# The results of two chunks go into the place of chunk 1's rows, and the third chunk is loaded meanwhile

## Chip, cores and metric

One core of one Trainium2 chip. The metric is the device time of one execution in microseconds; times of a kernel are medians over runs.

## What is computed

Three layers, cut to what matters here:

```python
def reference(q, k, v, w_in, w_out, w_gate, w1, w2):
    a = attn(q, k, v)              # 4 batches x 8 heads, 576 positions, width 64:
                                   # pooled attention (mean of 4) plus a band of |i-j| < 4
    x = a.transpose(0, 2, 1, 3).reshape(2304, 512)
    h = x @ w_in                   # 512 -> 2048
    g = np.where(h >= 1, h, np.where(h <= -1, 0.0, (h + 1) ** 2 / 4))
    x = g @ w_out                  # 2048 -> 512
    # then 8 experts with 288 rows each: the logits x @ w_gate, all of them
    # sorted, set which row goes to which expert
    return experts(x, w_gate, w1, w2)   # relu(x @ w1[e]) @ w2[e] for its rows
```

## The kernel before, in words

The program is written as many small generators (`pooled`, `local`, `prep`, `up`, `down`, `gates`, `flush` and so on). While the program is built, a planner in `run` keeps a modelled clock for each engine and lets the generator go on that is due first; what it yields says on which engine its next piece goes (`"P"` TensorE, `"A"` ScalarE, `"V"` VectorE, `"G"` GpSimd, `"N"` none) or what it has to wait for: a condition on marks (`done("x", c)`), a PSUM bank, or a named place (`need(..., "xio")`). `CAPS` says how many places of each name there are; of `xio` there is one. So the order of the instructions on each engine is fixed when the program is built, and on the chip an engine takes its instructions in that order and waits on semaphores. The order of SyncE is also that of all loads and stores (`dma`, L104 to L108).

All instructions of an engine are written by one helper each: L106 issues transfers, L120 matmuls, L124 transposes, L128 ScalarE, L141 VectorE and GpSimd.

In the first part of the run three things are interleaved: the attention (16 pairs of heads, `pooled` and `local`; its results are written to `x_cols` in DRAM, column by column), the preparation of the weights (`prep`, which splits each of 16 blocks of `w_in` and `w_out` into a high and a low part), and the second layer in chunks of 256 rows of x. The first seven chunks run here, two more go together behind them.

A chunk goes so. `load_chunks` loads its columns from `x_cols` into `xio` (L717) and splits them: ScalarE copies the high part into `xts` (L723), VectorE or GpSimd subtracts for the low part (`low_part`, L707). `xts` has two tiles, for even and odd chunks. `gemm1` then makes one of 16 blocks of h, 12 matmuls of 128x256 in one half of PSUM bank 0; `gates` makes g of it (two `gar` on ScalarE, then VectorE, GpSimd or both, then `ghi` and `glo`). The product with `w_out` follows.

Chunks 0 and 1 run side by side (`up` and `down`), since the weights come block by block: their results fill banks 1 to 4, two for each chunk. `flush_first` scales them into `xio` (L643 to L647), writes them to `x_rows`, transposes them, and computes the logits from them (`mark("logits", c)`); only at its end it gives `xio` back (L668). From chunk 2 on `gemm` drives the blocks: `gemm1` of block n and `gemm2` of block n - 2 (`LAG` at L40), whose results lie in banks 1, 2 and 3. `gemm2` of chunk c waits for `done("flush", c - 1)` (L764), so that of chunk 2 waits until chunk 1's banks have been emptied. `load_chunks` loads chunk 2 when chunk 0 has passed its 16 blocks and `xio` is free (L712).

After the chunks come the last rows, the routing, and the eight experts, which are not touched.

Of the kernel before, what the change touches and what calls it, by code (L numbers as in the profile page):

```python
# [11 lines left out]
F32 = mybir.dt.float32  # L12
F32R = mybir.dt.float32r
# [79 lines left out]
def body(ctx, tc, qk_d, v4_d, vw_d, win, wout, wg, w1, w2, cst_d, bits_d, out):  # L93
# [10 lines left out]
    def dma(out, x):  # L104

        nc.sync.dma_start(out, x)  # L106
        free["D"] = max(free["D"], cur[0] + DL[0]) + 4.0 * int(np.prod(out.shape)) / 360.0
        return free["D"] + DL[1] - cur[0]  # L108
# [4 lines left out]
    def mm(out, w, x, **kw):  # L113
        n = size(x)
        if x.dtype == F32:
            ns = max(4.0 * n / 2.4, 200.0 * (n == E)) if w.shape[0] > 72 else 80.0 * max(n, 32) / 64
        else:
            ns = max(w.shape[-1] / 1.2, n / (6.0 if w.shape[-1] == 32 else 2.4), 25.0)
        spend("P", cur[2] * ns)
        return nc.tensor.matmul(out, w, x, **kw)  # L120

    def transpose(out, x, i):
        spend("P", cur[2] * (2.0 * x.shape[0] / 2.4 + 3.0))
        return nc.tensor.transpose(out, x, i)  # L124

    def act(out, x, f, **kw):
        spend("A", {AF.Exp: 280.0, AF.Relu: 145.0}.get(f, 85.0) + 0.83 * size(x))
        return nc.scalar.activation(out, x, f, **kw)  # L128
# [15 lines left out]
    V = Engine("V", nc.vector, 65.0, 1.05)  # L144
# [12 lines left out]
    def bank(i):  # L157
        return PS.tile([128, 512], F32, name=nm("bk"), tag=f"b{i}")

    def pool_fn(pool):  # L160
        def f(shape, dt, name, bufs=1):
            return pool.tile(shape, dt, name=nm(name), tag=name, bufs=bufs)
        return f
# [31 lines left out]
    bt = pool_fn(GP.enter_context(tc.tile_pool(name="ffn", bufs=1)))  # L195
# [11 lines left out]
    spare, EXTRA = {"q4": [0], "pe": [0, 1], "paT": [0, 1]}, {}  # L207
# [10 lines left out]
    def spawn(gen, e="N", delay=0.0):  # L218
        put(gen, cur[0] + delay, e)
# [49 lines left out]
    def done(*k):  # L269
        return k[1] < 0 or k in flags  # L270

    def mark(*k):
        flags[k] = cur[0]

    def open_banks():
        return [b for b in banks if b > 4] if done("av", 3, RS) and not B0 else list(banks)

    def need(e, *names, cond=None, bank=0, temp=0):

        def f():  # L280
            few = [n for n in temps if n < (temp() if callable(temp) else temp)]
            if (cond and not cond()) or any(not room[n] for n in names) or len(open_banks()) < bank or (temp and not few):
                return None
            got = open_banks()
            got = got[:bank] if B0 else got[::-1][:bank]
            for b in got:
                banks.remove(b)
            return (got if bank > 1 else got[0] if bank else None, temps.pop(temps.index(max(few))) if temp else None,
                    *[room[n].pop(0) for n in names])
        f.engine = e  # L290
        return f
# [10 lines left out]
    def drop(bank=None, **names):  # L302
        for n, k in names.items():
            room[n].append(k)
            room[n].sort()
        if bank is not None:
            banks.append(bank)
            if not B0:
                banks.sort()
# [259 lines left out]
    XTS = {}  # L569
# [45 lines left out]
    FIRST = {}  # L615
# [11 lines left out]
    def down(c):  # L627
        for f in range(16):
            yield need("P", cond=lambda: done("gate", 16 * c + f) and done("prep", f, 0))
            hi, lo, kg = GG.pop((c, f))  # L630
            for t in range(2):
                x = FIRST["x"][2 * c + t]
                gh, gl = (g[:, t * 128:t * 128 + 128] for g in (hi, lo))
                mm(x, gh, WO[f][:, 0, 0:512], start=f == 0, stop=False)
                mm(x, gh, WO[f][:, 1, 0:512], start=False, stop=False)
                mm(x, gl, WO[f][:, 0, 0:512], start=False, stop=f == 15)
            drop(G=kg)
            yield "N"
        spawn(flush_first(c))

    def flush_first(c):
        yield need("V", "xio")
        xe = bt([128, 1024], F32, "xio").rearrange("p (t d) -> p t d", t=2)  # L643
        for t in range(2):
            x = FIRST["x"][2 * c + t]
            act(xe[:, t, 0:256], x[:, 0:256], AF.Copy, scale=1.0 / 256)
            V.tensor_scalar(xe[:, t, 256:512], x[:, 256:512], 1.0 / 256, None, op0=OP.mult)  # L647
        dma(xd[256 * c:256 * c + 256, :].rearrange("(t p) d -> p t d", p=128), xe)
        mark("flush", c)
        banks.extend(FIRST["b"][2 * c + t] for t in range(2) if FIRST["b"][2 * c + t] > 3)  # L650
        for t in range(2):
            b, _ = yield need("P", bank=1)
            ps = bank(b)
            for k in range(4):
                transpose(ps[:, 128 * k:128 * k + 128], xe[:, t, 128 * k:128 * k + 128], ident)
            _, _, kr = yield need("A", "rows")
            rows = at([128, 512], F32, f"rows{kr}")
            act(rows, ps, AF.Copy)
            drop(bank=b)
            b, _ = yield need("P", bank=1)  # L660
            pg = bank(b)[:, 0:E]
            for k in range(4):
                mm(pg, rows[:, 128 * k:128 * k + 128], wgk[:, k], start=k == 0, stop=k == 3)
            drop(rows=kr)
            yield "V"
            V.tensor_scalar(L[:, 2 * c + t, :], pg, 256.0, None, op0=OP.mult)
            drop(bank=b)
        drop(xio=0)  # L668
        mark("logits", c)

    def gemm2(c, f):
# [29 lines left out]
    def there(n):  # L701

        b, o = divmod(n - 1, S)
        return all(done("av", i, g) for i in range(4 * b + 4) for g in range(2) if i < 4 * b or g == 0 or o >= LO)

    def low_part(c, k, x, XT):
        yield from flex(dict(V=XL[0], G=XL[1]), XT[:, 1, k], x[:, k], f32(XT[:, 0, k]), OP.subtract)  # L707
        mark("xs", c, k)

    def load_chunks():  # L710
        for c in range(NC):
            yield need("N", "xio", cond=lambda: there(256 * c + 256) and (c > 1 or done("scored", 2 + c, 1)) and done("first", c - 2) and (c == 2 or done("flush", c - 2)) and (c or all(1 in spare[n] for n in ("pe", "paT"))))  # L712
            x = bt([128, 1024], F32, "xio").rearrange("p (k n) -> p k n", k=4)
            if c == 0:
                for n in ("pe", "paT"):
                    spare[n].remove(1)
            yield dma(x, xtd[:, :, 256 * c:256 * c + 256]) + XD  # L717
            if c < 2:
                XTS[c] = bt([128, 2, 4, 256], F32R, f"xts{c}")
            XT = XTS[c % 2]  # L720
            for k in range(4):
                yield "A"
                act(XT[:, 0, k], x[:, k], AF.Copy)  # L723
                spawn(low_part(c, k, x, XT))
            yield need("N", cond=lambda: all(done("xs", c, k) for k in range(4)))
            drop(xio=0)
            mark("x", c)
# [78 lines left out]
    for f in range(16):  # L806
        put(prep(1, f), 0.0)
        put(prep(0, f), 0.0)
    put(load_chunks(), 0.0)
    put(gemm(), 0.0)  # L810
    lt = None
# [50 lines left out]
    first = rt([1, E], BF, "first")  # L862
# [495 lines left out]
```

## Time and profile before

| | |
|---|---|
| median of 3 runs | 899.41 us (894.22 to 908.81) |
| the profiled execution | 900.66 us, of which 898.5 us are its span |
| TensorE busy | 858.7 us, 96% of the span |
| VectorE, ScalarE, GpSimd busy | 514.9, 463.1, 439.2 us |
| granted clock of TensorE, mean of the span | 0.98 |

The span runs from the first to the last instruction; times in the trace count from its start. A busy TensorE is not one at its peak, since matmuls overlap and their ends are modelled. The granted clock is TensorE's: 1.00 is 2.4 GHz, 0.50 is 1.2 GHz. "Idle before, with a releaser" is the time for which an engine stood still ahead of an instruction, and what ended it by the semaphores.

### The profile page before, as it was taken

How to read it: one execution, taken by the hardware profiler on the slowest of the kernel's cores; microseconds unless marked ns; L12 is line 12 of the kernel's file. 1: busy time of each engine (PE TensorE's matmuls, PEld its weight loads, DVE VectorE, ACT ScalarE, POOL GpSimd, SP SyncE). 2: the span in 40 equal slices, each digit the busy share in tenths (PEclk: the TensorE clock that was granted, in tenths of full speed). 3: DMA queues.
4: the chain of work that ended last, by engine and by line, in shares of the span. 5: the costliest groups of instructions: out<-in, count | busy, mean ns of one | idle time of the engine just before them, and what ended most of it. 6: DMA issues, size and time to landing. Idle time of an engine off the chain costs nothing.

```text
span 898.5 us, 20588 instructions
## 1 busy us (share of the span) xinstructions
PE 858.7 (96%) x7891; PEld 777.8 (87%) x7891; DVE 514.9 (57%) x1469; ACT 463.1 (52%) x1295; POOL 439.2 (49%) x498
## 2 busy tenths in 40 slices
PE   7879999989899999999999999998999999999995
PEld 6768888878899999999999877777988998989995
DVE  6788989876454543423221564475576766767520
ACT  5877786776466666544444551032343443544641
POOL 3765477654244544444444210033855756657741
PEclk9999999999899999999999999997999999999998
DMA  9755455223222310301000000053433544436620
GB/s 308 232 176 185 139 179 194 88 61 111 89 64 70 103 42 15 95 1 49 1 25 1 30 1 6 1 207 126 145 122 128 183 140 152 150 101 209 208 84 27
DMA packets 39010, 95.41 MB, mean 106 GB/s; under 512 B 4992, under 2 KB 17152, under 8 KB 38912
## 3 DMA queue, kind: packets, MB, share of 16 engines
q1 hardware_dynamic: 35840, 84.66, 28.8%
q0 software_dynamic: 3072, 9.44, 3.4%
q8 instruction: 62, 1.02, 0.5%
q14 instruction: 36, 0.29, 0.1%
HBM read 79.92 MB, written 14.16 MB: 105 GB/s over the span
## 4 chain that ended last, share of the span: by engine, by line
PE 72%; DVE 8%; DMA 7%; issue 5%; ACT 4%; POOL 2%; SPq 1%; POOLq 0%; DVEq 0%; ACTq 0%
PE bk L120 70%; PE bk L124 3%; DMA stg<-in_w_dram 2%; DVE gar L141 1%; DMA vw<-in_vw_dram 1%; ACT gar L128 1%; DVE raw L141 1%; DMA v<-in_v_dram 1%; DMA x_rows<-xio 1%; POOL wo L141 1%; DMA x_cols<-x 1%; POOL out_dram L1116 1%; SPq L106 1%; DVE t L141 1%; DMA xg<-x_rows,idx 1%
## 5 line engine op out<-in xcount | busy, mean ns | idle before, releaser
L120 PE MATMUL bk<-xts,wi 128*128 128x256 f32 x1344 | 184.8, 288 | 5.3 <-ACT gar L128 3.7
L120 PEld LDWEIGHTS bk<-xts,wi 128*128 128x128 f32 x1344 | 170.6, 192 | 9.4 <-ACT gar L128 5.1
L120 PE MATMUL bk<-wo,ghi 128*128 128x256 f32 (+2 forms) x768 | 161.8, 309 | 0.0
L128 ACT ACTIVATE gar<-bk,halves 128x256 f32<-128x256 f32 x224 | 93.8, 471 | 91.0 <-PE bk L120 85.4
L141 DVE SCALAR_TENSOR_TENSOR gar<-gar 128x256 f32<-128x256 f32 x112 | 57.4, 513 | 115.7 <-ACT gar L128 115.4
L120 PEld LDWEIGHTS bk<-wo,ghi 128*128 128x128 f32 x768 | 115.9, 190 | 4.6 <-issue 0.4
L141 POOL TENSOR_TENSOR glo<-gar,ghi 128x256 fp32r<-128x256 f32 x86 | 65.8, 771 | 86.4 <-ACT ghi L128 71.5
L141 POOL TENSOR_TENSOR wi<-stg,wi 128x512 fp32r<-128x512 f32 x51 | 64.7, 1297 | 69.4 <-DMA stg<-in_w_dram 43.0
L120 PE MATMUL bk<-wo,glo 128*128 128x256 f32 (+2 forms) x384 | 90.3, 303 | 0.2 <-DVE glo L141 0.2
L141 POOL TENSOR_TENSOR gar<-gar 128x256 f32<-128x256 f32 x64 | 49.6, 775 | 72.4 <-DVE gar L141 47.0
L141 POOL TENSOR_TENSOR wo<-stg,wo 128x512 fp32r<-128x512 f32 x50 | 65.6, 1335 | 37.6 <-ACT wo L128 37.3
L120 PEld LDWEIGHTS bk<-wo,glo 128*128 128x128 f32 x384 | 62.1, 189 | 3.6 <-DVE glo L141 0.9
L128 ACT ACTIVATE ghi<-gar 128x256 fp32r<-128x256 f32 x112 | 46.7, 417 | 34.9 <-POOL gar L141 19.5
L120 PE MATMUL bk<-xT,wi 128*128 128x288 f32 x384 | 60.8, 311 | 0.1
L120 PE MATMUL bk<-hT,wi 128*128 128x288 f32 x384 | 60.5, 304 | 0.0
L128 ACT ACTIVATE wi<-stg 128x1024 fp32r<-128x1024 f32 x32 | 33.6, 1056 | 51.4 <-DMA stg<-in_w_dram 51.4
L120 PE MATMUL bk<-hT,wo 128*128 128x288 f32 x384 | 58.8, 302 | 0.0
L120 PE MATMUL bk<-xT,wo 128*128 128x288 f32 x384 | 58.4, 302 | 0.1
L128 ACT ACTIVATE lt<-lt,lmx 128x64 f32<-128x64 f32 x160 | 53.8, 342 | 8.9 <-DVE lmx L141 8.7
L120 PEld LDWEIGHTS bk<-xT,wi 128*128 128x128 f32 x384 | 54.4, 197 | 0.8 <-DVE xT L141 0.3
L120 PEld LDWEIGHTS bk<-xT,wo 128*128 128x128 f32 x384 | 52.0, 188 | 1.0 <-DVE xT L141 0.6
L120 PEld LDWEIGHTS bk<-hT,wi 128*128 128x128 f32 x384 | 52.1, 188 | 0.7
(189 smaller groups left out, 1669.2 us busy)
## 6 DMA issues: line engine op xcount, KB each, us to landing
stg<-in_w_dram SPq DMA_DIRECT2D x64, 512.0 KB
qk<-in_qk_dram SPq DMA_DIRECT2D x14, 590.0 KB
raw<-in_win_dram SPq DMA_DIRECT2D x16, 512.0 KB
raw<-in_wout_dram SPq DMA_DIRECT2D x16, 512.0 KB
v<-in_v_dram SPq DMA_DIRECT2D x32, 144.0 KB
xio<-x_cols SPq DMA_DIRECT2D x7, 512.0 KB
x_rows<-xio SPq DMA_DIRECT2D x7, 512.0 KB
vw<-in_vw_dram SPq DMA_DIRECT2D x16, 192.0 KB
```

The lines of the kernel that those rows point to most:

```text
L106: nc.sync.dma_start(out, x)
L120: return nc.tensor.matmul(out, w, x, **kw)
L124: return nc.tensor.transpose(out, x, i)
L128: return nc.scalar.activation(out, x, f, **kw)
L141: return fn(out, *args, **kw)
L1116: return nc.gpsimd.indirect_dma_start(**kw)
```

## The change

Chunks 0 and 1 are flushed only when both have passed all their 16 blocks of `gemm1`. Their scaled results then go into one new tile in the place of chunk 1's `xts` (128x2048, half for each chunk) and not into `xio`, so `flush_first` neither takes nor gives back `xio`. Chunk 2 may be loaded into `xio` as soon as its columns are there; the copy into `xts` waits for the 16 blocks of chunk 0, whose place it takes. Chunk 3 is loaded when the logits of chunks 0 and 1 are done, and gets a new tile in the place that the results held.

```diff
     def flush_first(c):
-        yield need("V", "xio")
-        xe = bt([128, 1024], F32, "xio").rearrange("p (t d) -> p t d", t=2)
+        yield need("V", cond=lambda: done("first", 0) and done("first", 1))
+        if "e" not in FIRST:
+            FIRST["e"] = bt([128, 2048], F32, "xts1")
+        xe = FIRST["e"][:, 1024 * c:1024 * c + 1024].rearrange("p (t d) -> p t d", t=2)
         for t in range(2):
...
-        drop(xio=0)
         mark("logits", c)
...
     def load_chunks():
         for c in range(NC):
-            yield need("N", "xio", cond=lambda: there(256 * c + 256) and (c > 1 or done("scored", 2 + c, 1)) and done("first", c - 2) and (c == 2 or done("flush", c - 2)) and (c or all(1 in spare[n] for n in ("pe", "paT"))))
+            yield need("N", "xio", cond=lambda: there(256 * c + 256) and (c > 1 or done("scored", 2 + c, 1)) and (c == 2 or done("first", c - 2) and done("flush", c - 2)) and (c != 3 or done("logits", 0) and done("logits", 1)) and (c or all(1 in spare[n] for n in ("pe", "paT"))))
...
             yield dma(x, xtd[:, :, 256 * c:256 * c + 256]) + XD
-            if c < 2:
-                XTS[c] = bt([128, 2, 4, 256], F32R, f"xts{c}")
+            if c == 2:
+                yield need("N", cond=lambda: done("first", 0))
+            if c < 2 or c == 3:
+                XTS[c % 2] = bt([128, 2, 4, 256], F32R, f"xts{c % 2}")
```

The planner moves the pieces around these. On TensorE the two orders differ only between the last block of chunk 1 and the tenth block of chunk 2; ahead of and behind that stretch they are the same.

SyncE's queue where the load of chunk 2 stands now, before (rows 91 to 97; `raw` are weights, `vw` and `v` are for the attention):

```order
L106 DMA x_cols<-x_2134 128x348
L106 DMA vw_2139<-in_vw_dram 128x384
L106 DMA raw_2169<-in_win_dram 128x1024
L106 DMA raw_2171<-in_wout_dram 128x1024
L106 DMA x_cols<-x_2190 128x228
L106 DMA v_2196<-in_v_dram 72x512
L106 DMA v_2198<-in_v_dram 72x512
```

and after, rows 91 to 97:

```order
L106 DMA x_cols<-x_2134 128x348
L106 DMA xio_2139<-x_cols 128x4x256
L106 DMA vw_2141<-in_vw_dram 128x384
L106 DMA raw_2171<-in_win_dram 128x1024
L106 DMA raw_2173<-in_wout_dram 128x1024
L106 DMA x_cols<-x_2192 128x228
L106 DMA v_2198<-in_v_dram 72x512
```

The load of chunk 2 was row 111 and is row 92, right behind the write of the columns that it reads.

ScalarE at the last gates of chunks 0 and 1, before (`gar_2988` is the gate of chunk 0's last block, `gar_3038` that of chunk 1's, `xts_895<-xio` the copies of chunk 2):

```order
L128 ACTIVATE qpz_77<-q_2928 64x9x16 x2
L128 ACTIVATE ghi_2873<-gar_2875 128x256
L128 ACTIVATE rows_2972<-bk_2939 128x512
L128 ACTIVATE laT_2978<-bk_2948 128x256
L128 ACTIVATE ghi_2908<-gar_2910 128x256
L128 ACTIVATE gar_2988<-bk_941,halves 128x256 x2
L128 ACTIVATE wo_2935<-bk_2981 128x8
L128 ACTIVATE w2g<-bk_2981 128x8
L128 ACTIVATE pe_3020,psm_3008<-bk_2992,pmx_3007 96x144 x3
L128 ACTIVATE ghi_2986<-gar_2988 128x256
L128 ACTIVATE gar_3038<-bk_941,halves 128x256 x2
L128 ACTIVATE xts_895<-xio_2937 128x256 x4
```

and after (`gar_3003` is the gate of chunk 0's last block):

```order
L128 ACTIVATE xts_895<-xio_2139 128x256
L128 ACTIVATE qpz_77<-q_2930 64x9x16 x2
L128 ACTIVATE ghi_2875<-gar_2877 128x256
L128 ACTIVATE xts_895<-xio_2139 128x256
L128 ACTIVATE rows_2978<-bk_2939 128x512
L128 ACTIVATE xts_895<-xio_2139 128x256
L128 ACTIVATE ghi_2910<-gar_2912 128x256
L128 ACTIVATE laT_2993<-bk_2947 128x256
L128 ACTIVATE xts_895<-xio_2139 128x256
L128 ACTIVATE gar_3003<-bk_941,halves 128x256 x2
```

The four copies stood behind the gate of chunk 1's last block, and now stand, one by one, ahead of the gate of chunk 0's last block.

TensorE from the first block of chunk 2 to the start of its `gemm2`, before (`wi_422`, `wi_649` and `wi_723` are chunk 2's first three blocks, `cst,xio` the transposes of the flushed rows, `wgk,rows` their logits, `wo_641` the first `gemm2`):

```order
L120 MATMUL bk_941<-xts_895,wi_422 128x256 x12
L124 MATMUL bk_3149<-cst,xio_3122 128x128 x4
L120 MATMUL bk_941<-xts_895,wi_649 128x256 x12
L120 MATMUL bk_941<-xts_895,wi_723 128x256 x12
L120 MATMUL bk_3198<-wgk_84,rows_3176 128x8 x4
L124 MATMUL bk_3208<-cst,lt_0582_3067 128x128 x3
L124 MATMUL bk_3216<-cst,xio_3122 128x128 x4
L120 MATMUL bk_3233<-wgk_84,rows_3228 128x8 x4
L120 MATMUL bk_3239<-laT_3231,vw_2974 64x58 x12
...
L124 MATMUL bk_3280<-cst,xio_3254 128x128 x4
L120 MATMUL bk_3288<-wo_641,ghi_3168 128x256
```

and after (`wo_2937` with `ghi_3043` are the last products of chunk 1):

```order
L120 MATMUL bk_941<-xts_895,wi_422 128x256 x12
...
L120 MATMUL bk_941<-xts_895,wi_649 128x256 x12
L120 MATMUL bk_944<-wo_2937,ghi_3043 128x512 x2
L120 MATMUL bk_944<-wo_2937,glo_3044 128x512
L120 MATMUL bk_945<-wo_2937,ghi_3043 128x512 x2
L120 MATMUL bk_945<-wo_2937,glo_3044 128x512
...
L120 MATMUL bk_941<-xts_895,wi_723 128x256 x12
L120 MATMUL bk_3175<-wo_641,ghi_3082 128x256
```

Two blocks of chunk 2 now stand ahead of chunk 1's last products, the third is followed at once by chunk 2's first `gemm2`, and the transposes of the flushed rows come behind that.

## Rows read from the trace of the kernel before

**Rows 1.** The page, busy time of an engine, share of the span, instructions.

```profile
PE 858.7 (96%) x7891; PEld 777.8 (87%) x7891; DVE 514.9 (57%) x1469; ACT 463.1 (52%) x1295; POOL 439.2 (49%) x498
```

**Rows 2.** Busy time by stretch: length, engines' busy us (instructions), clock, DMA share, GB/s.

```profile
200.00:209.75 9.75, 9.39 (x98) 8.81 (x97) 8.21 (x14) 6.23 (x17) 5.94 (x7) 1.00 0.36 107
209.75:254.20 44.45, 40.94 (x399) 36.92 (x398) 22.41 (x61) 27.20 (x104) 15.25 (x21) 0.92 0.30 99
...
240.00:356.00 116.00, 116.00 (x1261) 110.36 (x1259) 57.95 (x141) 72.51 (x267) 53.03 (x72) 1.00 0.19 62
356.00:376.00 20.00, 19.43 (x163) 18.96 (x159) 10.08 (x22) 11.47 (x30) 8.00 (x11) 1.00 0.37 112
376.00:585.00 209.00, 209.00 (x1487) 185.74 (x1486) 73.40 (x194) 82.52 (x180) 62.98 (x77) 1.00 0.04 13
```

**Rows 3.** The waits of TensorE from 209 to 255 us: total, times, longest.

```profile
PE bk L120 <- ACT rows L128: 1.9, 1, 1.9
PE bk L120 <- ACT gar L128: 0.9, 1, 0.9
PE bk L120 <- ACT laT L128: 0.5, 1, 0.5
```

**Rows 4.** Busy time by stretch, in stretches of 2 us.

```profile
228.00:230.00 2.00, 0.12 (x1) 0.12 (x2) 1.48 (x4) 2.00 (x7) 1.19 (x3) 1.00 0.00 0
230.00:232.00 2.00, 2.00 (x22) 1.98 (x24) 0.63 (x3) 1.17 (x4) 1.47 (x3) 0.60 0.04 8
232.00:234.00 2.00, 1.47 (x20) 0.96 (x16) 0.72 (x2) 0.38 (x1) 1.84 (x4) 0.50 0.43 168
234.00:236.00 2.00, 2.00 (x21) 1.90 (x22) 0.40 (x1) 0.00 (x0) 0.31 (x1) 0.50 0.87 282
236.00:238.00 2.00, 2.00 (x15) 2.00 (x14) 0.00 (x0) 0.60 (x1) 0.00 (x0) 0.70 0.57 167
```

**Rows 5.** The timeline of TensorE: start us, us, what, [idle before it and releaser].

```profile
214.84 0.58 PE L120 MATMUL bk<-qk 64*64 64x64 f32 x24
...
219.23 0.40 PE L120 MATMUL bk<-wo,glo 128*128 128x512 f32 x1
...
220.20 1.70 PE L120 MATMUL bk<-xts,wi 128*128 128x256 f32 x12
...
229.88 1.45 PE L120 MATMUL bk<-wgk,rows 128*128 128x8 f32 x8 [1.95 <-ACT rows L128]
...
235.75 0.78 PE L120 MATMUL bk<-wo,ghi 128*128 128x256 f32 x2
```

**Rows 6.** The timeline of ScalarE and VectorE at the gates, copies and flushes.

```profile
209.84 0.84 ACT L128 ACTIVATE gar<-bk,halves 128x256 f32<-128x256 f32 x2
...
214.13 1.34 ACT L128 ACTIVATE xts<-xio 128x256 fp32r<-128x256 f32 x4
...
216.64 1.96 DVE L141 TENSOR_TENSOR xts<-xio,xts 128x256 fp32r<-128x256 f32 x4
...
219.22 0.64 ACT L128 ACTIVATE xio<-bk 128x256 f32<-128x256 f32 x2
...
230.99 0.64 ACT L128 ACTIVATE xio<-bk 128x256 f32<-128x256 f32 x2
```

**Rows 7.** The timeline of SyncE's queue and of ScalarE, 145 to 172 us.

```profile
145.36 0.33 SPq L106 DMA_DIRECT2D x_cols<-x  x1
...
171.89 0.69 ACT L128 ACTIVATE t<-raw 128x512 f32<-128x512 f32 x1
```

**Rows 8.** The chain that ended last, in order of time: start us, us, what.

```profile
52.77 4.36 DMA x_cols<-x
...
359.19 7.03 DMA x_rows<-xio
```

**Rows 9.** The timeline of GpSimd and VectorE at 178 us.

```profile
178.65 1.47 POOL L141 TENSOR_TENSOR wi<-t,wi 128x512 fp32r<-128x512 f32 x1
...
178.89 1.51 DVE L141 SCALAR_TENSOR_TENSOR gar<-gar 128x256 f32<-128x256 f32 x1
```

## The prediction

> **What bounds the kernel now.** I read the page first: TensorE is busy 858.7 us, 96% of the span of 898.5 us, and no other engine passes 57% [rows 1]. So time can only be won where TensorE waits or runs at its lower clock. The busy times by stretch tell where that is [rows 2]: from 240 to 356 us and from 376 to 585 us TensorE is busy every microsecond at a granted clock of 1.00. In the stretch that the change touches, 209.75 to 254.2 us, it is busy 40.94 of 44.45 us at 0.92. So 3.51 us are idle there, and some more is lost to the clock.
>
> The waits of that stretch name three stalls: 1.9 us for `rows` on ScalarE, 0.9 us for `gar` (a gate) on ScalarE, 0.5 us for `laT` [rows 3]. In the timeline the longest, 1.95 us, ends at 229.88 [rows 5]. At 228 to 230 TensorE works 0.12 us of 2; then the granted clock reads 0.60, 0.50, 0.50 and 0.70 in the next four windows, that is, it falls from the 2.4 to the 1.2 GHz level and is back at about 237 us [rows 4].
>
> Why does TensorE have so little to do there? Chunk 0's results are scaled into `xio` at 219.22, chunk 1's not before 230.99, although the products of both have ended by 219.63 [rows 5, 6]. The one place `xio` is held until chunk 0's logits are computed, and `gemm2` of chunk 2 may not start before chunk 1's banks are emptied: its first product stands at 235.75 [rows 5]. Meanwhile TensorE runs three blocks of chunk 2 and then pieces that wait for each other.
>
> **The change, part by part.** *The load of chunk 2* moves up SyncE's queue from behind row 110 to row 92, right behind the write of `x_cols` that it reads. SyncE holds the queue there until that write has landed. The write is issued at 145.36 [rows 7]; a write of `x_cols` on which the first chunk's load waited took 4.36 us on the chain [rows 8]. So the `vw`, the two `raw`, the next `x_cols` and the `v` behind it go out some 4.4 us late. The first of these `raw` is read at 171.89 [rows 7], 26 us later than the queue stops. Cost on the path: 0, and up to 26 us of delay would be needed before it has any.
>
> *The conversion of chunk 2* (four copies on ScalarE, four subtractions on VectorE) moves ahead. The copies took 1.34 us for four, the subtractions 1.96 us [rows 6]. The copies now stand ahead of the gate that began at 209.84, so that gate begins at 209.84 + 1.34 = 211.2, and the last subtraction ends near 211.2 + 0.49 = 211.7. TensorE comes to chunk 2's first block where the scores of a head stood before, at 214.84 [rows 5]: 3.1 us to spare. The gate that is 1.34 us late is read by products that now stand behind this block of 1.7 us (220.20 [rows 5]), so it is hidden too.
>
> *The flushes* no longer wait for `xio`. The last products of chunk 1 ended at 219.63 [rows 5]; now two blocks of chunk 2, 1.7 us each, stand ahead of them, so they end near 222.9 and chunk 1's results are scaled at about 223 instead of 230.99. `gemm2` of chunk 2 then follows the third block, near 224.5, instead of 235.75. Its first bank is free earlier still. The rows' transposes and the logits come behind it, two by two, with other work between each and its copy. This is what takes the three stalls away: TensorE has 12 products of `gemm2` per block to run where it waited. What is late next is nothing that the trace shows: all three stalls of [rows 3] have this cause, and behind them the next stretch has none.
>
> *The load of chunk 3* waits for both logits instead of `xio`. Its rows are wanted only behind chunk 2's sixteenth block, and TensorE is never idle up to there [rows 2]. Cost 0. The second write of `x_rows` goes out at about 224, ahead of the next `qk` load, which TensorE reads only behind the tenth block of chunk 2. Cost 0.
>
> **The sum.** TensorE's instructions are the same ones. Idle time removed: at most 3.51 us. Clock: the four windows from 230 to 238 lose 2 x (0.40 + 0.50 + 0.50 + 0.30) = 3.4 us of full speed; of this 0.27 fall on the 0.53 us that it stood idle in 232 to 234, so 3.1 us [rows 4]. Together 6.6 us, the upper bound. The Trainium skill ("TensorE: Matmul & The Clock Gate", Terms) puts the penalty at the throttled time times one minus the ratio of the clocks: 6.8 us at half speed make 3.4 us, and the sum would be 6.9 us; the rows' 3.1 differ by the idle part alone. New waits in the new order: at least none, at most all 6.6 us (nothing gained), or more in the rival below. I take the share of idle time of the unchanged stretch just ahead, 200 to 209.75 us: 0.36 of 9.75, or 3.7% [rows 2]; over the 38 us that remain of the stretch that is 1.4 us. Net gain 6.6 - 1.4 = 5.2 us.
>
> From the tenth block of chunk 2 on, TensorE's order is what it was. With TensorE busy all the time from 240 to 356 us, everything behind moves up with it. The profiled execution took 900.66 us, the median of three runs is 899.41; their middle is 900.0, and 900.0 - 5.2 = 894.8 us. One run can lie 1% off (894.22 to 908.81).
>
> **The rivals.**
>
> *The gain is absorbed (900 us).* The earlier stream runs into a point set by transfers: at 359.19 the chain holds 7.03 us of a write of `x_rows` [rows 8], and TensorE is busy 19.43 of 20 us there [rows 2]. If that chain kept its own pace, the stretch would grow by the 5.2 us. For it: here a transfer, not TensorE, ends last. Against it: the write and the loads in it are started by TensorE's own results, which all come 5.2 us earlier.
>
> *Slower (901.4 us): VectorE's subtractions slip.* They now stand where VectorE, ScalarE and GpSimd finish the last gates. VectorE can be slow there: a gate's operation took 1.51 us at 178.89 while GpSimd ran a subtraction of 1.47 us [rows 9], against 0.49 for one of the four here. The Trainium skill ("SBUF — State Buffer", Who interferes with whom) has a rule that speaks for this: a VectorE instruction with two SBUF inputs, as these are, contends with a GpSimd instruction that reads SBUF. The trace agrees as far as that row. Six operations of VectorE stand from the first of the four to the last. At 1.1 us more each, the last ends at 211.7 + 6.6 = 218.3, TensorE waits 3.5 us from 214.84 on and then runs at half speed as it did after 228 us, 3.1 us: 6.6 us lost, 5.2 gained, 900.0 + 1.4 = 901.4. It decides from the point where the last subtraction ends after 216.9 (2.1 us of waiting and 3.1 of clock eat 5.2 us), that is, at 0.87 us more per operation. Against it: the same four took 1.96 us in a stretch where GpSimd was busy too.
>
> *The change does not do what it says.* The order shows that it does: the load stands 19 rows higher on SyncE, and both flushes write one tile, `xts_3125`. What it can't show is when the load lands; between its issue near 150 us and the copies near 208 us lie more than 50 us, so I give this no chance.
>
> **How the numbers follow.** Forecast 894.8 with its own range 892 to 898: 0.66. Absorbed, 898 to 901: 0.15. Slower by VectorE's slip, 900 to 904: 0.12. Something else, 0.07. The range of eight in ten reaches from 889 (the whole 6.6 us and a median of three runs that falls 4 us low) to 902.5. A measurement of this kernel can tell about 2%, 18 us, from no change. No case comes near that, so within 2%: 0.93, faster 0.03, slower 0.04 for what I have not seen.
>
> **What would show it.** In the profile after: the copies of chunk 2 near 208 to 211 us, the first block of chunk 2 near 215 us without a wait, chunk 1's results scaled near 223 us, no window under 1.00 of granted clock between 210 and 250 us, and TensorE's blocks from the tenth of chunk 2 on some 5 us earlier, down to the end of the span. A stall at chunk 2's first block, or a shift of 5 us at 300 us that is gone at 380 us, would show the rivals. I am wrong if the shift at 260 us is under 2 us, or if the end moves by something that is not this shift.

## The result, and the profile after

The kernel after takes 890.45 us (median of 12 runs, 888.43 to 896.44), the kernel before 900.02 us (12 runs, 894.22 to 908.81). The ratio is 0.9904 with a 95% interval of 0.988 to 0.9929; by this ratio it takes 8.6 us less, 6.4 to 10.8. The forecast was 894.8 us, 5.2 us less. The result lies 1.6 us under the forecast's own range (892 to 898) and inside the wider one of 889 to 902.5; it is within 2% of the kernel before, to which the prediction gave 0.93. The profiled execution took 889.23 us, its span is 887.4 us against 898.5 us.

The page after, the rows that answer to [rows 1], and the span:

```profile
span 887.4 us, 20581 instructions
...
PE 853.0 (96%) x7891; PEld 773.3 (87%) x7891; DVE 512.1 (58%) x1467; ACT 463.4 (52%) x1295; POOL 442.2 (50%) x500
```

TensorE has the same 7891 instructions and is busy 5.7 us less; about 3.1 us of that is the dip of the clock in the changed stretch, which is gone (3.4 us in [rows 4], of which 0.27 fell on idle time). Another dip, between 606 and 624 us and so outside that stretch, cost 5.1 us in this profile of before and 1.7 us in this one of after. Busy time by stretch of the kernel after, as in [rows 2]:

```profile
200.00:209.75 9.75, 9.38 (x97) 9.02 (x96) 8.92 (x16) 6.63 (x19) 6.74 (x8) 1.00 0.19 57
209.75:254.20 44.45, 44.45 (x480) 40.51 (x480) 22.80 (x64) 29.91 (x111) 18.62 (x25) 1.00 0.31 102
...
356.00:376.00 20.00, 19.50 (x161) 19.08 (x160) 8.72 (x17) 11.22 (x28) 8.01 (x11) 1.00 0.16 56
376.00:585.00 209.00, 209.00 (x1470) 183.83 (x1469) 77.97 (x216) 82.96 (x177) 63.38 (x76) 1.00 0.06 20
```

In the changed stretch TensorE is now busy all 44.45 us at a clock of 1.00, with 480 instructions where there were 399. The timeline of TensorE in the kernel after:

```profile
206.88 1.61 PE L120 MATMUL bk<-xts,wi 128*128 128x256 f32 x12
...
213.52 1.59 PE L120 MATMUL bk<-xts,wi 128*128 128x256 f32 x12
...
220.07 0.39 PE L120 MATMUL bk<-wo,glo 128*128 128x512 f32 x1
...
220.78 1.68 PE L120 MATMUL bk<-xts,wi 128*128 128x256 f32 x12
222.30 0.41 PE L120 MATMUL bk<-wo,ghi 128*128 128x256 f32 x2
...
224.47 1.09 PE L124 MATMUL bk<-cst,xts 128*128 128x128 f32 x8
...
226.82 1.85 PE L120 MATMUL bk<-wgk,rows 128*128 128x8 f32 x16
...
347.42 0.67 PE L120 MATMUL bk<-laT,vw 64*64 64x58 f32 x16
```

Compare with [rows 5]: chunk 2's first block stands at 213.52 (220.20 before), ahead of chunk 1's last product at 220.07; the second GEMM of chunk 2 begins at 222.30 instead of 235.75; the transposes and logits of both chunks come in pairs, eight and sixteen instructions, and no row shows a wait.

One length serves to compare all runs. **T** is the time from chunk 1's last block of the first GEMM (206.88 above) to the last head's local attention (347.42): 140.54 us here. The same two rows of the kernel before:

```profile
208.09 1.66 PE L120 MATMUL bk<-xts,wi 128*128 128x256 f32 x12
...
355.46 0.67 PE L120 MATMUL bk<-laT,vw 64*64 64x58 f32 x16
```

T was 147.37 us, so this pair of profiles differs by 6.83 us in T, by 1.2 us ahead of it (208.09 against 206.88) and by 3.0 us behind it. Only T is the change's: the first experiment shows that the other two parts move by more than that without any edit. An end that moves by more than the shift was one of the prediction's signs of being wrong; it came in this pair, by what differs from run to run.

### The profile page after: what moved, and what is told of

It reads as the page before. It is cut to its first block, busy times and chain, and to the rows that moved or that the text cites. A ratio compares the mean times of both kernels' runs of the same rounds, so it can differ in the third digit from the quotient of the medians.

```text
span 887.4 us, 20581 instructions
## 1 busy us (share of the span) xinstructions
PE 853.0 (96%) x7891; PEld 773.3 (87%) x7891; DVE 512.1 (58%) x1467; ACT 463.4 (52%) x1295; POOL 442.2 (50%) x500
## 4 chain that ended last, share of the span: by engine, by line
PE 73%; DVE 8%; DMA 6%; issue 5%; ACT 3%; POOL 3%; SPq 1%; DVEq 0%; POOLq 0%; ACTq 0%
PE bk L120 70%; PE bk L124 3%; DMA stg<-in_w_dram 2%; DVE gar L141 1%; DMA vw<-in_vw_dram 1%; DVE raw L141 1%; POOL wo L141 1%; DMA v<-in_v_dram 1%; DMA x_rows<-xio 1%; DVE wi L141 1%; ACT gar L128 1%; DMA x_cols<-x 1%; POOL out_dram L1119 1%; DVE xT L141 1%; SPq L106 1%
## 5 line engine op out<-in xcount | busy, mean ns | idle before, releaser
L120 PE MATMUL bk<-xts,wi 128*128 128x256 f32 x1344 | 182.5, 285 | 3.3 <-ACT gar L128 2.7
L120 PEld LDWEIGHTS bk<-xts,wi 128*128 128x128 f32 x1344 | 168.6, 190 | 7.3 <-ACT gar L128 4.3
L141 POOL TENSOR_TENSOR gar<-gar 128x256 f32<-128x256 f32 x67 | 51.9, 774 | 75.4 <-DVE gar L141 50.6
```

Source lines behind the costliest of these rows:

```text
L141: return fn(out, *args, **kw)
```

## The experiments

The change has two halves: the **new place** for the flushes, in which both may stand side by side, and the **early rows**, chunk 2 loaded and converted sooner. The planner lays out each variant anew, so a run without one half also has another order of instructions. From "Without the filler" to "The kernel before again" each kernel ran once, so T of one profile is all that these runs give. What a run "won" is counted from the first profile of before, 147.37 us.

S, in the earlier expectations, is a longer stretch than T: it ends at the last chunk's first block.

**The kernel after again** (no edit).

> The kernel after, once more, for what differs from run to run. S is the time from the first product of chunk 1's last block of the first GEMM to the first product of the last chunk's first block (tile XTL); it is 282.64 us in the profile before and 275.69 in the one after, so 6.95 of the 11.1 us by which the spans differ lie in S, 1.2 ahead of it and 2.9 behind it. Theory (only S is the change's; the rest is run to run): S again 275.7 within 0.2; the time ahead of S and behind S moves by 1 us or more against the first profile, and the median lies 7 to 9 us under before. Rival (the change also shortens the part behind S, by 2 to 3 us): S 275.7 and the part behind S within 0.3 us of 404.8.

S 275.63 us, T 140.54 us, both as in the first profile of after to 0.1 us. Ahead of T it took 209.47 us and behind it 545.25 us, where the first profile of after has 206.88 and 540.02, and the kernel before 208.09 and 543.04. The theory holds: what differs outside T is run to run. Only its range for the median is missed: 893.27 us in four runs, ratio 0.9891 (0.9836 to 0.9947), which is 9.9 us under before and not 7 to 9, though the interval takes these in.

**The new place alone.**

```diff
-... and (c == 2 or done("first", c - 2) and done("flush", c - 2)) and ...
+... and done("first", c - 2) and (c == 2 or done("flush", c - 2)) and ...
...
-            if c == 2:
-                yield need("N", cond=lambda: done("first", 0))
```

> The flushes go into the new place, but chunk 2 is loaded and converted at its old point. Theory (the gain comes from the flushes that no longer wait for each other): S 276 to 278 us, no granted clock under 1.00 for more than 2 us in the stretch, time 5 to 7 us under before. Rival (it comes from having chunk 2's rows early): S 281 to 283 us, time within 1.5 us of before.

S 281.77, T 146.40 us: 0.97 us won, ratio 0.9982 (0.9945 to 1.0019). My theory falls. TensorE in this run:

```profile
218.29 1.58 PE L120 MATMUL bk<-xts,wi 128*128 128x256 f32 x12
219.81 0.71 PE L120 MATMUL bk<-paT,vs 72*64 72x144 f32 x8
220.45 1.66 PE L120 MATMUL bk<-xts,wi 128*128 128x256 f32 x12
221.95 0.60 PE L124 MATMUL bk<-cst,xts 128*128 128x128 f32 x4
223.10 1.68 PE L120 MATMUL bk<-xts,wi 128*128 128x256 f32 x12 [0.55 <-ACT gar L128]
224.62 0.60 PE L124 MATMUL bk<-cst,xts 128*128 128x128 f32 x4
226.26 1.06 PE L120 MATMUL bk<-wgk,rows 128*128 128x8 f32 x8 [1.04 <-ACT rows L128]
```

GpSimd, the last part of the first gate of chunk 2, in the same run:

```profile
226.59 0.73 POOL L141 TENSOR_TENSOR glo<-gar,ghi 128x256 fp32r<-128x256 f32 x1 [1.30 <-ACT ghi L128]
```

The flushes were early (transposes at 221.95), but chunk 2's first block came after chunk 1's last products, so its gate is finished at 227.3 only. Until then no product of the second GEMM can fill the waits of 0.55 and 1.04 us. Of the three stalls of [rows 3] the one for `laT` is gone here, and the other two are shorter.

**The early rows alone.**

```diff
-        yield need("V", cond=lambda: done("first", 0) and done("first", 1))
-        if "e" not in FIRST:
-            FIRST["e"] = bt([128, 2048], F32, "xts1")
-        xe = FIRST["e"][:, 1024 * c:1024 * c + 1024].rearrange("p (t d) -> p t d", t=2)
+        yield need("V", "xio")
+        xe = bt([128, 1024], F32, "xio").rearrange("p (t d) -> p t d", t=2)
...
+        drop(xio=0)
         mark("logits", c)
```

> Chunk 2 is loaded and converted early, but the flushes share one place that each holds until its logits are computed, as before. Theory (flushes): the three stalls and the clock dip come back, S 281 to 284 us, time within 1.5 us of before. Rival (early rows): S 276 to 278 us, time 5 to 7 us under before.

S 279.45, T 144.30 us: 3.07 us won, between the two theories. Ratio 0.9971 (0.9943 to 0.9998). Here the stall for `gar` is gone, that for `rows` is 0.75 us, and that for `laT` is left at 0.53 us.

**Both, but the flushes in turn.**

```diff
-        yield need("V", cond=lambda: done("first", 0) and done("first", 1))
+        yield need("V", cond=lambda: done("first", 0) and done("first", 1) and (c == 0 or done("logits", 0)))
```

> The kernel after in all, except that chunk 1's flush waits until chunk 0's logits are computed. Theory (flushes): S 281 to 284 us, like the run with the old place, with a stall of about 2 us and a granted clock of 0.5 behind it; time within 1.5 us of before. Rival (the new place itself or the early rows, not when the second flush starts): S 275.5 to 277 us and the time of the kernel after.

S 279.77, T 144.35 us, ratio 0.9966 (0.9938 to 0.9994). Both ranges for S are missed, the theory's (281 to 284) and the rival's (275.5 to 277), the stall is 0.75 us and not 2, and by the ratio the time is 3.1 us under before and not within 1.5; but T is that of the run with the old place to 0.05 us, as the theory had it. So it is not the place that counts but when the second flush starts. ScalarE in this run, chunk 0's flush and chunk 1's:

```profile
216.66 0.63 ACT L128 ACTIVATE xts<-bk 128x256 f32<-128x256 f32 x2
...
228.46 0.65 ACT L128 ACTIVATE xts<-bk 128x256 f32<-128x256 f32 x2
```

TensorE of the same run, from the stalls to the second GEMM:

```profile
226.75 1.06 PE L120 MATMUL bk<-wgk,rows 128*128 128x8 f32 x8 [0.75 <-ACT rows L128]
...
228.61 0.67 PE L120 MATMUL bk<-laT,vw 64*64 64x58 f32 x16 [0.53 <-ACT laT L128]
...
229.84 0.78 PE L120 MATMUL bk<-wo,ghi 128*128 128x256 f32 x2
```

Here the gates were ready and the banks were not: the second GEMM starts at 229.84, behind the stalls that it could have covered.

**Without the filler.**

```diff
-and (f > 0 or done("flush", c - 1)))
+and (f > 0 or done("flush", c - 1) and (c > 2 or done("logits", 1))))
```

> The kernel after in all, except that the second GEMM of chunk 2 waits for chunk 1's logits instead of for its flush alone. Theory A (chunk 2's products are the filler that covers the rows' copies): stalls of together over 1 us and a clock dip come back, S 278.5 to 280 us, as in the two runs with flushes one behind the other (279.45 and 279.77). Theory B (the stalls go because the transposes and logits of both chunks come together, eight and eight, and need no filler): no dip, S 275.5 to 276.5 us.

S 280.87, T 145.38 us: theory A, and 0.9 us beyond its range. Early rows and flushes side by side, but with the second GEMM held back two stalls return and most of the gain goes:

```profile
223.85 1.09 PE L124 MATMUL bk<-cst,xts 128*128 128x128 f32 x8
225.89 1.95 PE L120 MATMUL bk<-wgk,rows 128*128 128x8 f32 x16 [0.95 <-ACT rows L128]
227.70 1.07 PE L124 MATMUL bk<-cst,xts 128*128 128x128 f32 x8
229.14 3.58 PE L120 MATMUL bk<-wgk,rows 128*128 128x8 f32 x16 [0.37 <-ACT rows L128]
```

The second pair of logits takes 3.58 us, against 1.95 for the first, and 1.85 and 1.95 in the kernel after: it ran at the lower clock (0.67 and 0.50 in the windows from 228 to 232 us).

**VectorE's subtractions late, by 8 and by 16 more.**

```diff
     def low_part(c, k, x, XT):
+        if c == 2 and k == 3:
+            for _ in range(8):     # 16 in the second run
+                nc.vector.tensor_tensor(XT[:, 1, k], x[:, k], f32(XT[:, 0, k]), OP.subtract)
```

> The kernel after, with eight more subtractions on VectorE (each the same as chunk 2's last one, 0.33 us when they follow each other, 0.43 alone) ahead of chunk 2's last subtraction: it ends 2.6 to 3.4 us later. Theory (the rows were 3.1 us early, as 210.42 against 213.52 us shows): chunk 2's first block waits under 0.4 us, S 275.7 to 276.6 us. Rival (the gates behind them on VectorE have no such room): a stall of 0.5 to 1.5 us at chunk 1's last products, S 277 to 279 us.

> The same with sixteen: the last subtraction ends 5.3 to 6.9 us later. Theory (the price that the prediction's slower rival put on a slip: the wait beyond 3.1 us, and TensorE's clock at half behind it): chunk 2's first block waits 2 to 3.8 us, a granted clock of 0.5 behind it, S 279 to 283 us. Rival (a wait alone, no dip): S 277.5 to 279.5 us.

Eight took 3.64 us and sixteen 7.32 us, more than expected (at most 3.4 and 6.9). With eight, S is 277.27 and T 141.95 us, 1.41 more than after, with no dip, and chunk 2's block did not wait. The stall stands behind it, where transposes wait for `pe`, the pooled scores, which GpSimd scales with what VectorE computes behind the subtractions:

```profile
214.68 0.44 PE L124 MATMUL bk<-cst,pe 96*72 96x96 f32 x3 [1.04 <-POOL pe L141]
```

So the rival is right there, near the lower end of its range. With sixteen, T is 147.29 us, 6.75 more, and S 282.55, as the theory said. TensorE in that run:

```profile
213.24 1.36 PE L120 MATMUL bk<-xts,wi 128*128 128x256 f32 x10
217.55 0.80 PE L120 MATMUL bk<-xts,wi 128*128 128x256 f32 x2 [2.95 <-DVE xts L141]
```

The block starts on time and stops at its eleventh product, which is the first that needs the late part. The last subtraction ends 7.4 us later than in the kernel after and the block waits 2.95 us, so 4.4 us were hidden. The granted clock behind it reads 0.50 in the windows from 218 to 224 us.

**The dip of the clock by itself:** the kernel before, with useless products in its longest wait.

```diff
-            pg = bank(b)[:, 0:E]
+            pb = bank(b)
+            pg = pb[:, 0:E]
+            if (c, t) == (0, 1):
+                for _ in range(13):     # 8 in the second run
+                    nc.tensor.matmul(pb[:, 128:256], ident, ident, start=True, stop=True)
```

> The kernel before, with thirteen more products (128 x 128 by 128 x 128, 0.12 to 0.15 us each, of no use) ahead of the logits that waited 1.95 us for rows, so that TensorE works through that wait. Theory (the dip of the clock is a loss of its own, started by that wait, 3.1 us): no window under 1.00 behind it, S 279.3 to 280.5 us against 282.64. Rival (the dip comes from all the stalls of the stretch together, or costs nothing since the rows would be waited for): a dip all the same, S 282 to 283 us.

> The kernel before with eight useless products in place of thirteen in the wait of 1.95 us. Thirteen took 3.17 us, 0.244 each, and overran the wait by 1.14 us, so eight take 1.95 us and just fill it. Theory (the dip of the clock behind that wait is a loss of its own, of 2.8 to 3.1 us): no window under 1.00 between 228 and 240 us, T 144.3 to 144.7 us against 147.37. Rival (part of what the thirteen saved came from covering the wait with something else to do): T 145.3 us or more.

With thirteen, T is 145.64 us: 1.73 won, although the products overran the wait by some 1.1 us, and no window from 204 to 262 us is under 1.00. S does not show it (282.58, where 279.3 to 280.5 was expected), because further back, near 371 us, a stall of 2.0 us for `gar` stands in this run. With eight, T is 144.59 us, 2.78 won, inside the range of the theory. TensorE in that run:

```profile
227.20 2.05 PE L665 MATMUL bk<-cst 128*128 128x128 f32 x16
229.09 1.04 PE L120 MATMUL bk<-wgk,rows 128*128 128x8 f32 x8
```

TensorE does nothing of use sooner than before up to here; all that is won is the clock behind it (no window from 204 to 262 us is under 1.00). The waits of 0.93 and 0.53 us [rows 3] are still there and started no dip.

**The kernel before again** (no edit).

> The kernel before once more. From here on the stretch ends ahead of a stall near 370 us that differs from run to run: T is the time from the first product of chunk 1's last block of the first GEMM to the first product of the last head's local attention (laT by vw). T is 147.37 us in the profile before and 140.54 in the one after. Theory (T is set by the order of the work alone): 147.4 within 0.1, though the span may differ by several us. Rival (T differs from run to run like the rest): 146 to 149 us.

T 148.96 us: the rival, 1.6 us more than in the first profile. The waits are the same three (1.9, 0.9 and 0.5 us). The clock is not. Busy time in stretches of 2 us of this run:

```profile
228.00:230.00 2.00, 1.31 (x18) 1.29 (x20) 0.74 (x2) 1.54 (x5) 1.05 (x3) 1.00 0.00 0
230.00:232.00 2.00, 1.47 (x28) 1.00 (x24) 1.18 (x3) 0.82 (x3) 1.92 (x4) 0.63 0.09 31
232.00:234.00 2.00, 2.00 (x22) 1.90 (x21) 0.40 (x1) 0.08 (x1) 1.04 (x2) 0.50 0.98 329
234.00:236.00 2.00, 2.00 (x11) 2.00 (x11) 0.00 (x0) 0.52 (x1) 0.00 (x0) 0.50 0.76 229
236.00:238.00 2.00, 2.00 (x12) 2.00 (x11) 0.00 (x0) 0.00 (x0) 0.00 (x0) 0.50 0.20 75
238.00:240.00 2.00, 2.00 (x10) 2.00 (x11) 1.43 (x2) 0.00 (x0) 0.00 (x0) 0.50 0.00 0
240.00:242.00 2.00, 2.00 (x16) 2.00 (x16) 0.54 (x2) 1.15 (x3) 0.00 (x0) 0.81 0.00 0
```

The loss is 2 x (0.37 + 4 x 0.50 + 0.19) = 5.1 us, against 2 x (0.40 + 0.50 + 0.50 + 0.30) = 3.4 us in [rows 4].

**The same filling in the kernel after**, in two waits that it has left: behind the pooled scores of one head, and ahead of a routing round's count (round 0 in the first run, round 1 in the second).

```diff
...
+        if i == 9:
+            for _ in range(8):     # pb: the PSUM bank of the scores
+                nc.tensor.matmul(pb[:, 432:512], ident, ident[:, 0:80], start=True, stop=True)
         spare["q4"].append(kq)
...
+            if r == 0:     # r == 1 in the second run
+                for _ in range(5):     # bt_: the PSUM bank of the count
+                    nc.tensor.matmul(bt_[:, 128:256], ident, ident, start=True, stop=True)
             mm(tot, ones_bf, ac, start=True, stop=False)
```

> The kernel after, with useless products in two of the waits that are left and that a dip of the clock follows: eight (128 x 128 by 128 x 80) behind the pooled scores of the tenth head near 182 us, and five (128 x 128 by 128 x 128, 1.2 us) in the wait of 1.5 us ahead of the first round's count near 606 us. Theory (the clock falls because TensorE stands idle, so the dips go): no window under 0.9 at 184 to 188 us, saving up to 1.7 us; the dip near 608 us goes or shrinks, saving up to 1.6 us; time 1 to 3.5 us under the kernel after. Rival (other waits next to them bring the dips anyway, or the products delay what stands behind them): dips all the same, time within 1 us of the kernel after or above it.

> As the run before it, but the five products stand ahead of the second round's count, which is the one that waits 1.5 us near 606 us; in that run they stood ahead of the first round's, at 575 us, where TensorE was not idle. Theory (a dip of the clock near 608 us is started by this wait): the wait falls to 0.3 us or less and the dip, 1.6 us or more in each profile so far, goes or shrinks below 1 us; median 1 to 3 us under the kernel after. Rival (TensorE's short pieces and the gathers' waits ahead of it, from 602 us on, start the dip anyway): a dip all the same, and a median within 1.5 us of the kernel after.

The dip behind the pooled scores goes in both runs (no window under 1.00 from 184 to 192 us). Round 0 was the wrong one: its count runs at 575 us, where TensorE is not idle, and the wait of 1.5 us at 611 us and the dip stayed. With round 1 the wait shrinks and no window from 590 to 640 us is under 1.00 (1.7 us lost there in the first profile of after, 3.4 in the second):

```profile
608.62 1.38 PE L979 MATMUL bk<-cst 128*128 128x128 f32 x10
610.18 0.17 PE L120 MATMUL bk<-ac,cb 128*128 128x8 bf16 x1 [0.18 <-DVE ac L141]
```

The times are 893.69 us (ratio to before 0.991, 0.9878 to 0.9941) and 891.46 us (0.990, 0.9864 to 0.9935), those of the kernel after within what these runs can tell. The two fillings do what they should where they stand; that they make a faster kernel is not shown.

## Why the prediction was right, and where it was not

Set the sums beside T, from the windows of 2 us between 210 and 256 us (idle: 2 minus busy; clock: 2 times one minus the granted clock):

| run | T, us | over after | idle | clock |
|---|---|---|---|---|
| after, both profiles | 140.54 | 0 | 0 | 0 |
| before | 147.37 | 6.83 | 3.5 | 3.4 |
| before again | 148.96 | 8.42 | 3.5 | 5.1 |
| new place alone | 146.40 | 5.86 | 1.7 | 3.4 |
| early rows alone | 144.30 | 3.76 | 1.5 | 1.7 |
| flushes in turn | 144.35 | 3.81 | 1.5 | 1.7 |
| no filler | 145.38 | 4.84 | 1.3 | 3.4 |

Idle and clock together give the whole difference to 0.8 us or less in every row. The idle time of before falls by about half with either half of the change and to nothing with both. What sets the new place alone (0.97 us won) apart from the early rows alone (3.07) is the dip, 3.4 against 1.7 us, in one profile each; their ratios to before, 0.9982 and 0.9971, do not tell them apart.

- **What bounds the kernel: right. The upper bound of 6.6 us: none.** The three stalls and the dip are gone. The gain in T is 6.83 us from the first profile of before and 8.42 us from the second, both above the bound, which took its dip from one execution.
- **New waits, 1.4 us: the term that failed.** It was taken from the idle share of the stretch ahead, 3.7%. Measured: 0.00 us, 44.45 of 44.45 busy. A share of a neighbouring stretch said nothing of this one.
- **The clock, 3.1 us: one draw of a cost that varies.** It was read from one dip of one execution. The second profile of before lost 5.1 us behind the same waits. With both profiles the gain in T is 6.8 to 8.4 us, which holds with the measured 8.6 (6.4 to 10.8). This term and the new waits erred the same way, so nothing cancelled. The Trainium skill ("TensorE: Matmul & The Clock Gate", Terms) puts the penalty at the throttled time times one minus the ratio of the clocks; the trace of the second profile agrees: the 5.1 us reckoned so and 3.5 idle make 8.6, and T says 8.42.
- **Why the stalls go: half right.** The prediction put all three down to the one `xio` and priced the early conversion of chunk 2 at no gain. Neither half of the change takes all three away: the stall for `gar` goes with the early rows, that for `laT` with the new place, and that for `rows` only with both. The filler, which the prediction named (12 products per block where TensorE waited), needs both: chunk 2's gates, which the early rows bring, and chunk 1's banks, which the second flush frees. With both halves in place, holding that filler back costs 4.84 us, 3.4 us of it in the dip of one profile.
- **The load and its hold on SyncE: right at no cost.** The hold was forecast at 4.4 us, from a misread row: the write of 4.36 us at 52.77 [rows 8] was issued behind the first chunk's load (52.10) and is not the one that this load waited for. The queue of the kernel after issues the load 1.9 us behind the write that it reads:

```profile
144.12 0.33 SPq L106 DMA_DIRECT2D x_cols<-x  x1
146.01 0.53 SPq L106 DMA_DIRECT2D xio<-x_cols  x1
```

- **The conversion: right to 0.2 us.** VectorE's last subtraction of chunk 2 in the kernel after, which runs 1.2 us ahead of the kernel before at this point:

```profile
209.99 0.43 DVE L141 TENSOR_TENSOR xts<-xio,xts 128x256 fp32r<-128x256 f32 x1
```

ScalarE of the same run, the gate behind the copies and the two parts of chunk 1's flush:

```profile
209.81 0.83 ACT L128 ACTIVATE gar<-bk,halves 128x256 f32<-128x256 f32 x2
...
219.90 0.39 ACT L128 ACTIVATE xts<-bk 128x256 f32<-128x256 f32 x1
220.50 0.38 ACT L128 ACTIVATE xts<-bk 128x256 f32<-128x256 f32 x1 [0.21 <-PE bk L120]
```

The gate was forecast at 211.2, less 1.2 is 210.0; it begins at 209.81. The last subtraction was forecast to end at 211.7, less 1.2 is 210.5, and ends at 210.42. TensorE comes at 213.52: 3.1 us to spare, as forecast. To the eleventh product, the first that needs this part, it was 4.4 us, as the slip of sixteen showed. Chunk 1's results are scaled from 219.90 on and the second GEMM begins at 222.30; forecast were 223 and 224.5, less 1.2, so they come 1.9 and 1.0 us sooner.
- **Slower by VectorE's slip: no loss.** Of the six operations of VectorE from the first subtraction to the last, one did slip. In the kernel after:

```profile
207.93 0.95 DVE L141 TENSOR_TENSOR gar<-gar 128x256 f32<-128x256 f32 x1
```

and GpSimd beside it:

```profile
207.70 0.90 POOL L141 TENSOR_TENSOR glo<-gar,ghi 128x256 fp32r<-128x256 f32 x1 [1.07 <-ACT ghi L128]
```

It ended 0.28 us behind GpSimd's instruction; in the kernel before the same operation took 0.41 us at 208.86, with GpSimd idle. The Trainium skill's rule ("SBUF — State Buffer", Who interferes with whom) is that a VectorE instruction with two SBUF inputs, as this one is, contends with a GpSimd instruction that reads SBUF; the trace agrees with it in this row. It cost VectorE 0.5 us and TensorE nothing. The rival's price was near: it had 6.6 us lost for a slip of 6.6 us, and a slip of 7.4 us cost 6.75 us. Its point was not: it put the first loss at TensorE's block, and a slip of 3.7 us cost 1.41 us with the block not waiting at all, by the pooled scores behind it on VectorE.
- **Absorbed: did not happen.** The write of `x_rows` took 6.97 us (7.03 before) and is issued 3.73 us after the end of T in both (351.15 and 347.42; 359.19 and 355.46), so it moves with TensorE:

```profile
351.15 6.97 DMA x_rows<-xio
```

## What to carry to other kernels

Where an engine waits on a chain of short steps, look for what else it could run there and list everything that this filler needs: here either condition alone left half of the idle time and a dip behind it, and only both took the dip away. A wait on TensorE costs its own length and the dip behind it, if one follows; here a dip cost more (3.4 and 5.1 us) than the wait of 1.95 us ahead of it. One profile of a dip is one draw, so read it in two or three executions before it becomes a term. Useless products in a wait tell the two costs apart.

## Not expected of the hardware

- The same waits in the same kernel were followed by a dip that cost 3.4 us once and 5.1 us once. Waits of 0.75 and 0.53 us were followed by a dip in one kernel (flushes in turn, 1.7 us lost), waits of 0.93 and 0.53 us in another were not (eight useless products between them).
- A write of `x_rows` near 355 us took 6.85 to 7.03 us in all ten profiles of kernels without useless products on TensorE, and 8.2 to 8.4 us in the four with them, wherever these stood (at 227 us, or at 185 and beyond 570). From the end of T to the last chunk's first block it took 135.1 to 135.5 us in the four profiles of before and after, 136.4 to 138.4 us in those four, so they gave back 1 to 3 us of what they had won. Near the end of the longer write, in the three profiles in which this was read, the traffic falls to 7 to 27 GB/s for 1.3 to 1.6 us. The cause stays open.
- In the kernel before, where two blocks of the first GEMM stand close together, the gate of the first starts only when the second has ended (223.71):

```profile
223.74 0.84 ACT L128 ACTIVATE gar<-bk,halves 128x256 f32<-128x256 f32 x2 [1.81 <-PE bk L120]
```

The first block had ended at 221.9 [rows 5]. In the kernel after, products stand between the blocks and the gates of chunk 2's first four blocks start within 0.2 us of their block's end. Whether the chip or the program's own order makes the first gate wait stays open.
